# Attention in rounds of four heads: turning half a round ahead, three shared two-bank places, last keys' scores as four 64x64 tiles, segments of one tiling each

## The chip, the cores and the metric

The kernel runs on one core of a Trainium2 chip. The metric is the device time of one execution in microseconds (us), as the median of several runs. A core has five engines that run their own queues of instructions in order: PE (matrix products and transposes, writing PSUM), DVE (vector work), ACT (activations and copies), POOL (vector work that reads and writes SBUF) and SP, which here only issues DMAs. PSUM has eight banks of 512 floats per partition.

## The reference, cut to what matters

The program is an attention layer with a sigmoid in place of a softmax, followed by two dense layers. The change is in the attention alone.

```python
q, k, v: (4 batches, 12 heads, 448 positions, 64)      # float32
scores = scale * np.matmul(q, k.transpose(0, 1, 3, 2)) - np.log(S)
attn = 1.0 / (1.0 + np.exp(-scores))
x = np.matmul(attn, v)          # heads side by side: (1792, 768)
x = square(relu(x @ w_in)) @ w_out                      # 768 -> 2048 -> 768
x = (max(h, 0) + alpha * min(h, 0)) @ w2_out, h = x @ w2_in
```

The weights arrive as 64-bit floats and are turned into 32-bit ones on the chip.

## The kernel before

**Units and rounds.** A unit u is a pair of heads of one batch; there are 24. Two units, u and w = u + 1, make one pass of the attention loop, called a round here, so there are twelve rounds d = 0 to 11. The 448 keys of a head are three blocks of 128 (r or j = 0 to 2) and a rest of 64.

**Steps of a unit.** `fetch(u)` issues eight DMAs on SP: two each of q and k into the tile `nat`, the last 64 positions of q and k into `qk`, and v into `v` and `vrem`. `turn(u)` transposes q and k with seven matmuls against an identity into one two-bank PSUM tile `tp`; DVE then rounds it into `qkh` (L154) and takes the remainder into `qkl` (L155), so that hi and lo parts together carry full precision. `scores(u, j)` (L165) makes the scores of one block of 128 keys: three products (hi by hi, lo by hi, hi by lo), each for both heads, which are two row halves of the array side by side, a pair of matmuls. For the rest of 64 keys (j = 3) the same three pairs run with 128 columns of weights, of which half are of use. ACT applies the sigmoid to each two-bank result (L174), to `a`, or for the rest to `ar`, which two units share. `values(u, j)` (L183) multiplies the float32 sigmoids of a block with v: the two heads are two column halves of the array, and each float32 matmul stands as two records in the trace. `last_values(d)` (L192) does it for the rests of both units, as four 64x64 tiles at once. `finish(u)` copies the result out of PSUM as `xh` (ACT, L204) and `xl` (DVE, L205), in one or two pieces.

**PSUM.** One place of two banks for `tp`, two places of two banks for scores `sc`, two banks for `av`.

**Order.** The program's order is written by hand and each engine keeps it. In a round PE does two blocks of scores, a block or two of values, a turn, and so on, in eleven segments of one kind each. `turn` of a unit stands directly ahead of the previous unit's last two score blocks, and its DVE work is needed one segment pair later. `finish` of both units stands after `last_values`, ahead of the next turn's DVE work on DVE's queue.

**Weights in the attention.** From round 4 on, `assemble(i)` (ACT L82, DVE L83 to L85) and `split(i-1)` (ACT L95, POOL L96) prepare the first six weight tiles at the round's end, and `split` issues the load of a further tile on SP. The dense layers (L256, L289) follow when the attention is done, and PE works through them without a gap.

Of the kernel before, what the change touches and what calls it, by code (L numbers as in the profile page):

```python
# [9 lines left out]
F32 = mybir.dt.float32  # L10
# [9 lines left out]
def fused_kernel(ctx: ExitStack, tc: tile.TileContext, q, k, v, w1i, w1o, w2i, w2o, alpha, out):  # L20
# [53 lines left out]
    def assemble(i):  # L74

        if i >= len(items):
            return  # L80
        low, high = raws[i][:, :, 0], raws[i][:, :, 1]
        nc.scalar.activation(high.bitcast(F32), high.bitcast(F32), AF.Copy, scale=2.0 ** -112)  # L82
# [26 lines left out]
    with tc.manual_schedule():  # L109
# [5 lines left out]

        with tc.tile_pool(name="apool", bufs=1) as apool, tc.tile_pool(name="apsum", bufs=1, space=bass.MemoryType.PSUM) as psum:
            units = [(b, c) for b in range(B) for c in range(H // 2)]
            NAT = 3
            nats, qks, vals, vrems, parts, sig, avs = {}, {}, {}, {}, {}, {}, {}

            def fetch(u):
                if u >= len(units):
                    return
                b, c = units[u]
                hs = slice(2 * c, 2 * c + 2)
                nats[u] = apool.tile([P, 2, R, 2, D], F32, tag="nat", name=f"nat{u}", bufs=NAT)
                vals[u] = apool.tile([P, 2, R, D], F32, tag="v", name=f"v{u}", bufs=NAT + 1)
                qks[u] = apool.tile([P, 2, D], F32, tag="qk", name=f"qk{u}", bufs=NAT)
                if u % 2 == 0:
                    vrems[u // 2] = apool.tile([P, 2, D], F32, tag="vrem", name=f"vrem{u}", bufs=3)  # L130
                for j, src in enumerate((q, k, v)):
                    if j == 2:
                        nc.sync.dma_start(out=vals[u], in_=src[b, hs, :MAIN, :].rearrange("h (p r) d -> p h r d", r=R))
                    else:
                        for h in range(2):
                            nc.sync.dma_start(out=nats[u][:, j, :, h, :], in_=src[b, 2 * c + h, :MAIN, :].rearrange("(p r) d -> p r d", r=R))
                    last = (qks[u][:REM], qks[u][REM:], vrems[u // 2][half(u)])[j]
                    nc.sync.dma_start(out=last, in_=src[b, hs, MAIN:, :].rearrange("h p d -> p h d"))

            def half(u):  # L140
                return slice(u % 2 * REM, (u % 2 + 1) * REM)

            def turn(u):

                if u >= len(units):
                    return
                ps = psum.tile([P, 1024], F32, tag="tp", name=f"tp{u}", bufs=1)
# [5 lines left out]
                parts[u] = [apool.tile([P, 2 * S], F32R, tag=f"qk{part}", name=f"qk{part}{u}", bufs=2) for part in "hl"]  # L153
                nc.vector.tensor_copy(parts[u][0], ps[:, :2 * S])  # L154
                nc.vector.tensor_sub(parts[u][1], ps[:, :2 * S], parts[u][0])  # L155

            def scores(u, j):

                hi, lo = parts[u]
                at = 512 + j * P if j < R else S - u % 2 * REM  # L160
                ps = psum.tile([P, 2, 512], F32, tag="sc", name=f"sc{u}_{j}", bufs=2)
# [4 lines left out]
                if j < R:  # L166
                    a = sig[u, j] = apool.tile([P, 2, S], F32, tag="a", name=f"a{u}_{j}", bufs=6)
                    at = slice(0, P)
                else:
                    if u % 2 == 0:  # L170
                        sig[u // 2] = apool.tile([P, 2, S], F32, tag="ar", name=f"ar{u}", bufs=2)
                    a = sig[u // 2]
                    at = half(u)
                nc.scalar.activation(a[at], ps[at, :, :S], AF.Sigmoid, bias=bias[at], scale=SCALE)  # L174

            def values(u, j):
                if u < 0:
                    return
                if j == 0:
                    avs[u] = psum.tile([P, 512], F32, tag="av", name=f"av{u}", bufs=2)  # L180
                a, w = sig.pop((u, j)), vals[u]
                for h in range(2):
                    nc.tensor.matmul(avs[u][h * D:(h + 1) * D, :S], w[:, h, j, :], a[:, h, :], start=(j == 0), stop=False)  # L183

            def last_values(d):

                if d < 0:
                    return
                a, w = sig.pop(d), vrems.pop(d)
                for h in range(2):  # L190
                    for u in (2 * d, 2 * d + 1):
                        nc.tensor.matmul(avs[u][h * D:(h + 1) * D, :S], w[half(u), h, :], a[half(u), h, :], start=False, stop=True)  # L192
                finish(2 * d)
                finish(2 * d + 1)

            def finish(u):
                b, c = units[u]
                ps = avs.pop(u)
                for t, (first, n) in enumerate(TILES):
                    lo, hi = max(first, b * S), min(first + n, (b + 1) * S)  # L200
                    if lo < hi:
                        xh, xl = (p[:, lo - first:hi - first] for p in x_tiles(0, t, c))
                        part = ps[:, lo - b * S:hi - b * S]
                        nc.scalar.activation(xh, part, AF.Copy)  # L204
                        nc.vector.tensor_sub(xl, part, xh)  # L205

            fetch(0)
            fetch(1)
            nc.sync.dma_start(out=al, in_=alpha.rearrange("(f p) -> p f", p=P))
            turn(0)  # L210
            for u in range(0, len(units), 2):
                w = u + 1
                scores(u, 0)
                scores(u, 1)
                values(u - 1, 2)
                last_values(u // 2 - 1)
                fetch(u + 2)
                turn(w)
                scores(u, 2)
                scores(u, R)  # L220
                values(u, 0)
                values(u, 1)
                scores(w, 0)
                scores(w, 1)
                values(u, 2)
                fetch(u + 3)
                turn(u + 2)
                scores(w, 2)
                scores(w, R)
                values(w, 0)  # L230
                values(w, 1)

                i = u // 2 - 4
                if u in (2, 4, 6):
                    load(u // 2 - 1)
# [4 lines left out]
            values(len(units) - 1, 2)  # L240
            last_values(len(units) // 2 - 1)


        gpool = ctx.enter_context(tc.tile_pool(name="gpool", bufs=1, reuse_waits="tile"))
# [127 lines left out]
```

## Time and profile before

| what | number |
|---|---|
| median of 3 runs | 1127.27 us (1127.04 to 1127.32) |
| the profiled execution, its own time | 1126.52 us |
| its span in the trace | 1124.7 us |
| PE busy | 1098.4 us, 98% of the span |
| DVE, ACT, POOL busy | 676.2, 361.3, 152.6 us |
| start of the dense layers' first matmul on the chain | 184.56 us |
| granted TensorE clock of the core | 1.00 |

The span is what the trace covers; the execution's own time is 1.8 us more. Busy time is summed over stages with different limits, so the attention (0 to 184.56 us) has to be read by itself.

### The profile page before, as it was taken

To read this page: it belongs to the slowest core of one execution; us is meant where nothing else is said; L and a number is where in the kernel's file an instruction comes from. 1 tells how busy PE (TensorE), PEld (TensorE's weight loads), DVE (VectorE), ACT (ScalarE), POOL (GpSimd) and SP (SyncE) were. 2 spreads that over 40 slices of the span, in tenths; PEclk is the share of its full clock that TensorE was granted. 3 is DMA by queue.
4 is the path that set the end of the run, shared out by engine and by line. 5 is a ranking of instruction groups with operands and counts; after the bars stand their busy time and mean duration, and the time that the engine had idled before them with its cause. 6 is when DMAs were issued, how large, how long until landed. Compare 5 with 4: busy or idle time off the path is not lost.

```text
span 1124.7 us, 14542 instructions
## 1 busy us (share of the span) xinstructions
PE 1098.4 (98%) x5928; PEld 948.1 (84%) x5928; DVE 676.2 (60%) x967; ACT 361.3 (32%) x536; POOL 152.6 (14%) x94
## 2 busy tenths in 40 slices
PE   7999999999999999999999999999999999999998
PEld 4554546898989898989898999999989898989998
DVE  2446662246666666666665765567676767677554
ACT  4667665452322222222224443212121202121110
POOL 0001010010111111111114540102020202010000
PEclk9999999999999999999999999999999999999999
DMA  5763661011121112111212020202020201110014
GB/s 111 174 145 78 155 147 37 1 57 57 57 57 57 57 57 57 57 57 48 66 32 82 29 84 29 85 29 84 26 74 14 84 29 62 51 57 29 1 57 140
DMA packets 89267, 73.31 MB, mean 65 GB/s; under 512 B 52592, under 2 KB 83312, under 8 KB 89200
## 3 DMA queue, kind: packets, MB, share of 16 engines
q1 hardware_dynamic: 89200, 72.38, 22.7%
q8 instruction: 47, 0.77, 0.3%
q14 instruction: 20, 0.16, 0.0%
HBM read 66.85 MB, written 5.51 MB: 64 GB/s over the span
## 4 chain that ended last, share of the span: by engine, by line
PE 87%; DVE 8%; ACT 4%; issue 1%; SPq 0%; DMA 0%; ACTq 0%
PE h L256 39%; PE o L289 38%; PE sc L165 4%; PE av L183 3%; DVE raw L85 2%; DVE raw L84 2%; DVE xl L205 1%; ACT raw L82 1%; DVE qkl L155 1%; DVE qkh L154 1%; ACT xh L204 1%; DVE r L266 1%; DVE g L267 1%; PE tp L149 1%; ACT gh L268 1%; PE av L192 1%
## 5 line engine op out<-in xcount | busy, mean ns | idle before, releaser
L256 PE MATMUL h<-xh,wl 128*128 128x512 f32 (+1 forms) x768 | 278.5, 363 | 0.0
L256 PE MATMUL h<-xl,wh 128*128 128x512 f32 (+1 forms) x768 | 278.3, 362 | 0.0
L256 PE MATMUL h<-xh,wh 128*128 128x512 f32 (+1 forms) x768 | 277.9, 362 | 0.0
L294 DVE TENSOR_TENSOR acc<-o,acc 128x384 f32<-128x384 f32 (+1 forms) x364 | 200.0, 583 | 76.9 <-PE o L289 75.4
L96 POOL TENSOR_TENSOR wl<-raw,wh 128x768 fp32r<-128x768 f32 x64 | 122.3, 1911 | 899.6 <-ACT wh L95 828.9
L256 PEld LDWEIGHTS h<-xh,wh 128*128 128x128 f32 x768 | 144.2, 188 | 15.6 <-issue 0.7
L289 PE MATMUL o<-wh,gh 128*128 128x384 f32 x448 | 150.6, 336 | 6.5 <-DVE acc L294 6.2
L256 PEld LDWEIGHTS h<-xh,wl 128*128 128x128 f32 x768 | 144.1, 188 | 15.1
L256 PEld LDWEIGHTS h<-xl,wh 128*128 128x128 f32 x768 | 144.1, 188 | 15.0
L289 PE MATMUL o<-wl,gh 128*128 128x384 f32 x448 | 149.9, 335 | 0.0
L289 PE MATMUL o<-wh,gl 128*128 128x384 f32 x448 | 149.8, 334 | 0.0
L289 PE MATMUL o<-gh,wl 128*128 128x512 f32 (+1 forms) x384 | 139.1, 362 | 0.0
L289 PE MATMUL o<-gl,wh 128*128 128x512 f32 (+1 forms) x384 | 139.0, 362 | 0.0
L289 PE MATMUL o<-gh,wh 128*128 128x512 f32 (+1 forms) x384 | 138.9, 362 | 0.0
L268 ACT ACTIVATE gh<-g 128x512 fp32r<-128x512 f32 (+1 forms) x64 | 37.0, 579 | 284.8 <-DVE g L267 284.8
L269 DVE TENSOR_TENSOR gl<-g,gh 128x512 fp32r<-128x512 f32 (+1 forms) x128 | 93.2, 728 | 52.6 <-ACT gh L268 45.7
L95 ACT ACTIVATE wh<-raw 128x768 fp32r<-128x768 f32 x64 | 57.3, 895 | 174.9 <-DVE raw L85 129.0
L263 DVE SCALAR_TENSOR_TENSOR g<-h,r 128x512 f32<-128x512 f32 (+1 forms) x64 | 39.9, 623 | 112.7 <-ACT r L262 112.7
L84 DVE SCALAR_TENSOR_TENSOR raw<-raw 128x768 int32<-128x768 int32 x64 | 81.0, 1266 | 36.2 <-ACT raw L82 32.3
L262 ACT ACTIVATE r<-h 128x512 f32<-128x512 f32 (+1 forms) x64 | 34.8, 543 | 184.9 <-PE h L256 184.3
L289 PEld LDWEIGHTS o<-wh,gh 128*128 128x128 f32 x448 | 84.1, 188 | 9.3 <-DVE acc L294 8.1
L174 ACT ACTIVATE a<-sc,bias 128x896 f32<-128x896 f32 x72 | 70.0, 1005 | 51.9 <-PE sc L165 51.5
(44 smaller groups left out, 1185.1 us busy)
## 6 DMA issues: line engine op xcount, KB each, us to landing
raw<-in_moe_w_in_dram SPq DMA_DIRECT2D x32, 768.0 KB, 4.8
raw<-in_moe_w_out_dram SPq DMA_DIRECT2D x32, 768.0 KB, 4.4
nat<-in_q_dram SPq DMA_DIRECT2D x48, 96.0 KB, 3.2
nat<-in_k_dram SPq DMA_DIRECT2D x48, 96.0 KB, 2.9
v<-in_v_dram SPq DMA_DIRECT2D x24, 192.0 KB, 2.8
out_dram<-acc SPq DMA_DIRECT2D x16, 192.0 KB, 2.7
out_dram<-acc SPq DMA_DIRECT2D x6, 384.0 KB, 2.3
qk<-in_q_dram SPq DMA_DIRECT2D x24, 32.0 KB, 2.6
```

The costliest lines, as they stand in the source:

```text
L84: nc.vector.scalar_tensor_tensor(out=low, in0=high, scalar=3, in1=low, op0=ALU.logical_shift_left, op1=ALU.bitwise_or)
L95: nc.scalar.activation(hi, w, AF.Copy)
L96: nc.gpsimd.tensor_sub(lo, w, hi)
L165: nc.tensor.matmul(ps[:, h, :S], kt[rows, at:at + P], qt[rows, :S], start=(i == 0), stop=(i == 2))
L174: nc.scalar.activation(a[at], ps[at, :, :S], AF.Sigmoid, bias=bias[at], scale=SCALE)
L256: nc.tensor.matmul(ps[:, :n], wp[:, c * P:(c + 1) * P], xp, start=(c == 0 and i == 0), stop=(c == NC - 1 and i == 2))
L262: nc.scalar.activation(r, ps[:, :n], AF.Relu)
L263: nc.vector.scalar_tensor_tensor(out=gt, in0=ps[:, :n], scalar=0.0, in1=r, op0=ALU.max, op1=ALU.mult)
L268: nc.scalar.activation(gh, gt, AF.Copy)
L269: nc.vector.tensor_sub(gl, gt, gh)
L289: nc.tensor.matmul(ps[:, :size], *ops, start=(i == 0), stop=(i == len(turns) - 1))
L294: nc.vector.tensor_add(part, ps[:, :size], part)
```

## The change

The attention is written anew as rounds of two units. The main points, in the words of the code:

- `fetch(d)` loads both units of a round; it is issued for round d + 2 in the middle of round d, behind both turns. `nat` and `qk` have two places in place of three.
- `turn` of both units of round d + 1 stands in the middle of round d. DVE copies the transposes out of PSUM as float32 (`flat`), and makes the hi part (`part`) and the lo part (`rest`) later from this SBUF copy.
- The scores of the last 64 keys of four heads are one group, `last_scores(d)`: four float32 matmuls straight from `flat`, each in its own 64x64 tile, and one sigmoid of 128x896 in place of two of 64x896.
- One PSUM tag `big` of three two-bank places serves turns and scores alike, nine uses a round.
- `values(u)` does all three blocks at once. A round is last scores and last values, three blocks of scores, three of values, two turns, three of scores, three of values.
- `assemble` is cut in two: its ACT part stands in round i + 4, its DVE part (`step` 1) at the head of the next round.

```diff
-                nc.vector.tensor_copy(parts[u][0], ps[:, :2 * S])
-                nc.vector.tensor_sub(parts[u][1], ps[:, :2 * S], parts[u][0])
+                flats[u] = apool.tile([P, 2 * S], F32, tag="flat", name=f"flat{u}", bufs=2)
+                nc.vector.tensor_copy(flats[u], ps[:, :2 * S])
+            def part(u):
+                parts[u] = [apool.tile([P, 2 * S], F32R, tag=f"qk{p}", name=f"qk{p}{u}", bufs=3) for p in "hl"]
+                nc.vector.tensor_copy(parts[u][0], flats[u])
+            def rest(u):
+                nc.vector.tensor_sub(parts[u][1], flats[u], parts[u][0])
...
+            def last_scores(d):
+                ps = big(f"scr{d}").rearrange("p (h s) -> p h s", h=2)
+                for h in range(2):
+                    rows = slice(h * D, (h + 1) * D)
+                    for u in (2 * d, 2 * d + 1):
+                        nc.tensor.matmul(ps[half(u), h, :S], flats[u][rows, S:S + REM], flats[u][rows, :S], start=True, stop=True)
+                sig[d] = apool.tile([P, 2, S], F32, tag="ar", name=f"ar{d}", bufs=2)
+                nc.scalar.activation(sig[d], ps[:, :, :S], AF.Sigmoid, bias=bias, scale=SCALE)
...
+            for d in range(ND):
+                u, w = 2 * d, 2 * d + 1
+                i = d - 4
+                last_scores(d)
+                if d:
+                    last_values(d - 1)
+                    finish(u - 2)
+                if 0 < i < 7:
+                    assemble(i - 1, 1)
+                for j in range(R):
+                    scores(u, j)
+                if d:
+                    values(w - 2)
+                if d + 1 < ND:
+                    turn(u + 2)
+                    turn(w + 2)
+                    fetch(d + 2)
+                if d:
+                    finish(w - 2)
+                if d + 1 < ND:
+                    part(u + 2)
+                    rest(u + 2)
+                    part(w + 2)
+                    rest(w + 2)
+                if d in (1, 2, 3):
+                    load(d - 1)
                 if 0 <= i < 6:
-                    assemble(i)
+                    assemble(i, 0)
                 if 0 < i < 7:
                     split(i - 1)
+                for j in range(R):
+                    scores(w, j)
+                values(u)
+            last_values(ND - 1)
+            finish(2 * ND - 2)
+            values(2 * ND - 1)
+            finish(2 * ND - 1)
```

On PE, this is the program before, around the last keys' scores of unit 9 (`sc9_3`, three pairs) and the values that follow; a number behind a name is the unit, then the block.

```order
L165 MATMUL sc9_2_811<-qkh9_741 128x448 x2
L165 MATMUL sc9_2_811<-qkl9_742,qkh9_741 128x448 x2
L165 MATMUL sc9_2_811<-qkh9_741,qkl9_742 128x448 x2
L165 MATMUL sc9_3_820<-qkh9_741 128x448 x2
L165 MATMUL sc9_3_820<-qkl9_742,qkh9_741 128x448 x2
L165 MATMUL sc9_3_820<-qkh9_741,qkl9_742 128x448 x2
L183 MATMUL av9_828<-a9_0_775,v9_639 64x448 x2
L183 MATMUL av9_828<-a9_1_784,v9_639 64x448 x2
L165 MATMUL sc10_0_837<-qkh10_807 128x448 x2
```

The same place of PE in the changed program, the head of round 5: `scr5` are the last keys' scores of units 10 and 11, L204 the last values of round 4.

```order
L196 MATMUL av8_831<-a8_2_738,v8_486 64x448 x2
L186 MATMUL scr5_838<-flat10_754 64x448
L186 MATMUL scr5_838<-flat11_764 64x448
L186 MATMUL scr5_838<-flat10_754 64x448
L186 MATMUL scr5_838<-flat11_764 64x448
L204 MATMUL av8_831<-ar4_700,vrem4_484 64x448
L204 MATMUL av9_845<-ar4_700,vrem4_484 64x448
L204 MATMUL av8_831<-ar4_700,vrem4_484 64x448
L204 MATMUL av9_845<-ar4_700,vrem4_484 64x448
L176 MATMUL sc10_0_859<-qkh10_795 128x448 x2
L176 MATMUL sc10_0_859<-qkl10_796,qkh10_795 128x448 x2
```

Twelve matmuls for the last keys of two units (three pairs each) have become four, beside the last values, which use tiles of the same size.

On DVE, this is one weight round before, from the turn of unit 12 to the turn of unit 13 and its parts.

```order
L154 CAST qkh12_959<-tp12_951 128x896
L155 TENSOR_TENSOR qkl12_960<-tp12_951,qkh12_959 128x896
L83 TENSOR_SCALAR raw1_537<-raw1_537 128x768
L84 SCALAR_TENSOR_TENSOR raw1_537<-raw1_537 128x768
L85 SCALAR_TENSOR_TENSOR raw1_537<-raw1_537 128x768
L205 TENSOR_TENSOR xl0_0_4_564<-av10_915,xh0_0_4_563 128x64
L205 TENSOR_TENSOR xl0_1_4_1022<-av10_915,xh0_1_4_1021 128x384
L205 TENSOR_TENSOR xl0_0_5_568<-av11_980,xh0_0_5_567 128x64
L205 TENSOR_TENSOR xl0_1_5_1028<-av11_980,xh0_1_5_1027 128x384
L154 CAST qkh13_1051<-tp13_1043 128x896
L155 TENSOR_TENSOR qkl13_1052<-tp13_1043,qkh13_1051 128x896
```

The same round of DVE in the changed program, from the finish of unit 10 on.

```order
L215 TENSOR_TENSOR xl0_1_4_1005<-av10_983,xh0_1_4_1004 128x384
L86 TENSOR_SCALAR raw1_519<-raw1_519 128x768
L87 SCALAR_TENSOR_TENSOR raw1_519<-raw1_519 128x768
L88 SCALAR_TENSOR_TENSOR raw1_519<-raw1_519 128x768
L159 COPY flat14_1052<-tp14_1044 128x896
L159 COPY flat15_1062<-tp15_1054 128x896
L215 TENSOR_TENSOR xl0_0_5_648<-av11_997,xh0_0_5_647 128x64
L215 TENSOR_TENSOR xl0_1_5_1090<-av11_997,xh0_1_5_1089 128x384
L164 CAST qkh14_1093<-flat14_1052 128x896
L167 TENSOR_TENSOR qkl14_1094<-flat14_1052,qkh14_1093 128x896
L164 CAST qkh15_1097<-flat15_1062 128x896
L167 TENSOR_TENSOR qkl15_1098<-flat15_1062,qkh15_1097 128x896
```

The parts now stand last, read SBUF alone, and are for units of the round after; the finish of the second unit has come to stand behind both copies `flat`.

## Rows read from the trace of the kernel before

**Rows 1.** Page, busy us and share of the span by engine, with instructions

```profile
PE 1098.4 (98%) x5928; PEld 948.1 (84%) x5928; DVE 676.2 (60%) x967; ACT 361.3 (32%) x536; POOL 152.6 (14%) x94
```

**Rows 2.** Chain that ended last, 0 to 330 us: start, us, engine, tile, line

```profile
26.47 0.91 PE av L192 x8
...
28.30 1.42 PE sc L165 x12
29.71 1.65 PE av L183 x8
...
32.78 0.90 PE av L183 x4
...
39.98 0.91 PE av L192 x8
...
67.03 0.98 PE av L192 x8
...
171.66 0.98 PE av L192 x8
...
181.24 2.40 PE av L183 x12
...
184.56 16.54 PE h L256 x72
```

**Rows 3.** The same chain in the round from 67 us on

```profile
68.50 0.50 ACT xh L204
...
73.01 1.29 PE sc L165 x8
```

**Rows 4.** Timeline of PE, 28 to 42 us: start, us, line, operation, tiles

```profile
28.74 0.36 PE L165 MATMUL sc<-qkh,qkl 64*128 64x448 f32 x2
28.94 0.37 PE L165 MATMUL sc<-qkh 64*128 64x448 f32 x2
...
33.61 0.55 PE L149 MATMUL tp<-eye,nat 128*128 128x128 f32 x3
34.00 0.27 PE L150 MATMUL tp<-eye,qk 128*128 128x128 f32 x1
34.10 0.49 PE L152 MATMUL tp<-eye,nat 128*128 128x128 f32 x3
34.53 0.47 PE L165 MATMUL sc<-qkh 64*128 64x448 f32 x2
```

**Rows 5.** Timeline of DVE, 60 to 125 us

```profile
81.01 0.96 DVE L85 SCALAR_TENSOR_TENSOR raw<-raw 128x768 int32<-128x768 int32 x1
...
90.62 1.09 DVE L154 CAST qkh<-tp 128x896 fp32r<-128x896 f32 x1 [3.20 <-PE tp L152]
...
95.48 2.53 DVE L85 SCALAR_TENSOR_TENSOR raw<-raw 128x768 int32<-128x768 int32 x1
```

**Rows 6.** Timeline of POOL, 60 to 195 us

```profile
95.34 1.85 POOL L96 TENSOR_TENSOR wl<-raw,wh 128x768 fp32r<-128x768 f32 x1 [94.04 <-ACT wh L95]
```

**Rows 7.** Timeline of ACT, 80 to 115 us

```profile
88.25 1.91 ACT L174 ACTIVATE a<-sc,bias 128x896 f32<-128x896 f32 x2 [1.77 <-PE sc L165]
...
94.36 0.91 ACT L95 ACTIVATE wh<-raw 128x768 fp32r<-128x768 f32 x1
```

**Rows 8.** Timelines of SP's DMA queue: start, us to issue

```profile
21.33 0.62 SPq L138 DMA_DIRECT2D qk<-in_k_dram  x1
...
102.95 1.23 SPq L136 DMA_DIRECT2D nat<-in_q_dram  x2
...
107.51 0.62 SPq L138 DMA_DIRECT2D vrem<-in_v_dram  x1
```

**Rows 9.** DMA issues, 20 to 180 and 58 to 66 us: KB, median us to landing

```profile
qk<-in_k_dram SPq DMA_DIRECT2D x21, 32.0 KB, 2.9
...
nat<-in_q_dram SPq DMA_DIRECT2D x3, 96.0 KB, 5.0
```

**Rows 10.** Timeline of PE near the start

```profile
13.12 0.84 PE L152 MATMUL tp<-eye,nat 128*128 128x128 f32 x3
```

More of the change, by code (lines that the diff above doesn't have):

```diff
@@ L72, in load, with assemble @@
             nc.sync.dma_start(out=d, in_=w[f * P:(f + 1) * P, :])
-    def assemble(i):
+    def assemble(i, step=None):
         if i >= len(items):
@@ L81, in assemble @@
         low, high = raws[i][:, :, 0], raws[i][:, :, 1]
-        nc.scalar.activation(high.bitcast(F32), high.bitcast(F32), AF.Copy, scale=2.0 ** -112)
+        if step != 1:
+            nc.scalar.activation(high.bitcast(F32), high.bitcast(F32), AF.Copy, scale=2.0 ** -112)
+        if step == 0:
+            return
         nc.vector.tensor_scalar(out=low, in0=low, scalar1=29, scalar2=None, op0=ALU.logical_shift_right)
@@ L117, in fused_kernel @@
             units = [(b, c) for b in range(B) for c in range(H // 2)]
[L118 to L138, printed above, removed]
@@ L140, in half, with fetch @@
+            ND = len(units) // 2
+            nats, qks, vals, vrems, flats, parts, sig, avs = {}, {}, {}, {}, {}, {}, {}, {}
             def half(u):
                 return slice(u % 2 * REM, (u % 2 + 1) * REM)
+            def fetch(d):
+                if d >= ND:
+                    return
+                vrems[d] = apool.tile([P, 2, D], F32, tag="vrem", name=f"vrem{d}", bufs=3)
+                for u in (2 * d, 2 * d + 1):
+                    b, c = units[u]
+                    hs = slice(2 * c, 2 * c + 2)
+                    nats[u] = apool.tile([P, 2, R, 2, D], F32, tag="nat", name=f"nat{u}", bufs=2)
+                    vals[u] = apool.tile([P, 2, R, D], F32, tag="v", name=f"v{u}", bufs=5)
+                    qks[u] = apool.tile([P, 2, D], F32, tag="qk", name=f"qk{u}", bufs=2)
+                    for j, src in enumerate((q, k, v)):
+                        if j == 2:
+                            nc.sync.dma_start(out=vals[u], in_=src[b, hs, :MAIN, :].rearrange("h (p r) d -> p h r d", r=R))
+                        else:
+                            for h in range(2):
+                                nc.sync.dma_start(out=nats[u][:, j, :, h, :], in_=src[b, 2 * c + h, :MAIN, :].rearrange("(p r) d -> p r d", r=R))
+                        last = (qks[u][:REM], qks[u][REM:], vrems[d][half(u)])[j]
+                        nc.sync.dma_start(out=last, in_=src[b, hs, MAIN:, :].rearrange("h p d -> p h d"))
@@ L143, in turn, with big @@
+            def big(name):
+                return psum.tile([P, 1024], F32, tag="big", name=name, bufs=3)
             def turn(u):
-                if u >= len(units):
-                    return
-                ps = psum.tile([P, 1024], F32, tag="tp", name=f"tp{u}", bufs=1)
+                ps = big(f"tp{u}")
                 for r in range(R):
@@ L165, in scores @@
                         nc.tensor.matmul(ps[:, h, :S], kt[rows, at:at + P], qt[rows, :S], start=(i == 0), stop=(i == 2))
[L166 to L181, printed above, removed]
-                for h in range(2):
-                    nc.tensor.matmul(avs[u][h * D:(h + 1) * D, :S], w[:, h, j, :], a[:, h, :], start=(j == 0), stop=False)
+                sig[u, j] = apool.tile([P, 2, S], F32, tag="a", name=f"a{u}_{j}", bufs=5)
@@ L185, in last_values, with values @@
+            def values(u):
+                for j in range(R):
+                    a = sig.pop((u, j))
+                    if u % 2 == 0 and j == 0:
+                        avs[u] = psum.tile([P, 512], F32, tag="av", name=f"av{u}", bufs=2)
+                    for h in range(2):
+                        nc.tensor.matmul(avs[u][h * D:(h + 1) * D, :S], vals[u][:, h, j, :], a[:, h, :], start=(u % 2 == 0 and j == 0), stop=(u % 2 == 1 and j == R - 1))
             def last_values(d):
-                if d < 0:
-                    return
@@ L189, in last_values @@
-                a, w = sig.pop(d), vrems.pop(d)
+                a, w, u = sig.pop(d), vrems.pop(d), 2 * d
+                avs[u + 1] = psum.tile([P, 512], F32, tag="av", name=f"av{u + 1}", bufs=2)
                 for h in range(2):
[L191 to L194, printed above, removed]
+                    for i in (u, u + 1):
+                        nc.tensor.matmul(avs[i][h * D:(h + 1) * D, :S], w[half(i), h, :], a[half(i), h, :], start=(i > u), stop=(i == u))
@@ L209, in fused_kernel @@
[L209 to L235, printed above, removed]
+            nc.sync.dma_start(out=al, in_=alpha.rearrange("(f p) -> p f", p=P))
@@ new lines, in fused_kernel @@
+            for u in (0, 1):
+                turn(u)
+                part(u)
+                rest(u)
+            fetch(1)
+            for d in range(ND):
[24 more added lines that the diff above has]
+                    load(d - 1)
@@ L236, in fused_kernel @@
                 if 0 <= i < 6:
-                    assemble(i)
+                    assemble(i, 0)
                 if 0 < i < 7:
                     split(i - 1)
-            values(len(units) - 1, 2)
-            last_values(len(units) // 2 - 1)
+                for j in range(R):
+                    scores(w, j)
[4 more added lines that the diff above has]
+            finish(2 * ND - 1)
         gpool = ctx.enter_context(tc.tile_pool(name="gpool", bufs=1, reuse_waits="tile"))
```

13 lines of the change are left out of this document (7 added, 6 removed).

## The prediction

> **What bounds the kernel now.** I read the page first, then the chain that ended last, then the engines' timelines in the attention. PE is busy for 98% of the span [rows 1], so time is won only where PE gets less to do or waits less. The chain shows both kinds of loss in the attention. From 26.47 to 39.98 us it runs on PE alone: a whole round between two blocks of last values, 13.51 us without a wait [rows 2]. From 67.03 to 171.66 us there are seven rounds, 104.63 us, where seven of 13.51 would be 94.6; so about 10.1 us there are waits. Their pattern is seen after 68 us: PE has finished the last values, the chain leaves PE for the copies out of `av` on ACT and DVE and the parts of the next turn, and PE's scores return to it at 73.01 [rows 3]. The dense layers start at 184.56 [rows 2]; nothing behind that is edited, and I take it as unchanged. The question is when they start.
>
> **PE's work in a round.** All on PE, so all of it on the path. Before, a segment of two score blocks (six pairs) is 1.41 us from its start to the next segment, two blocks of values are 1.66, one is 0.90, the last values are 0.91 [rows 2], a turn is 0.92, from 33.61 to 34.53 [rows 4]. A round has four, two, two, one and two of these: 5.64 + 3.32 + 1.80 + 0.91 + 1.84 = 13.51, which is the round that the chain shows.
>
> Inside a segment a pair of score matmuls comes 0.20 us after the one before, and a transpose 0.10 to 0.11 after the one before [rows 4]. So 6 pairs are 1.2 us, and 0.2 is the change from one tiling to the next. After, a block of scores adds three pairs to a segment: 1.41 + 0.61 = 2.02. Three blocks of values are 2.40 us as the chain has them at 181.24 [rows 2]. Two turns in one segment are 0.92 + 7 x 0.107 = 1.67. The last values stay 0.91.
>
> The four float32 matmuls of the last keys' scores are not in the trace of before. The nearest row is that of the last values: four float32 matmuls of 64x64 tiles on 448 columns, eight records, 0.91 us with the change of tiling [rows 2]. The upper bound is that they run one after another. A block of values, two matmuls side by side, adds 1.65 - 0.90 = 0.75 us, so four in a row would be 3.0. Shape and type are those of the last values, and I take 0.76, behind which the last values follow in the same tiling: 0.91 + 0.76 = 1.67 for both. The round is then 1.67 + 2 x 2.02 + 2 x 2.40 + 1.67 = 12.18 us, or 1.33 less. About 0.46 of this is the last keys' scores (six pairs, 1.22 us, become 0.76), and the rest is five fewer changes of segment.
>
> **Waits that the new order makes.** Let t be the end of the first turn of a round. DVE copies it until t + 1.1 (a copy of 128x896 out of PSUM is 1.09 us [rows 5]) and the second until t + 2.2. PE needs 0.75 for the second turn and 1.3 for the next two blocks of scores (six pairs and the change of tiling), and the third block wants the PSUM place of the second turn: PE is there at t + 2.05, and waits about 0.2. I charge this in the ten rounds 1 to 10.
>
> In the weight rounds 5 to 9, ACT has a longer queue. The finish of the second unit goes copy, remainder, copy; its first remainder stands on DVE behind both `flat` copies, at t + 2.2. A whole finish takes 1.4 us (two of them and two passes of 1.09 fill the time from 68.01, the end of the last values, to 73.01 [rows 2, 3, 5]); of this ACT still needs some 0.75, with a copy of 0.50 in it [rows 3], and is through at t + 2.95. Then come two weight passes of 0.9 [rows 7] and the first sigmoid of the second unit, about 1.0 (two are 1.91 [rows 7]). That ends at t + 5.8. The next round's last scores take the PSUM place of this sigmoid; PE comes to it at t + 0.75 + 2.02 + 0.2 + 2.40 = t + 5.4. So another 0.4 or so of wait in five rounds; I take 0.45. In rounds 1 to 4 and 10 one or both weight passes are missing and it is hidden. Behind a waiting PE nothing is lost on other engines but their own idle time.
>
> **What lies beside PE.** Two sigmoids of 64x896 become one of 128x896, a sigmoid's time less on ACT each round, hidden anyway. DVE had four passes of 1.09 a round for two turns and now has six, two `flat` copies out of PSUM and four parts out of SBUF: 2.2 us a round more at most. In the light rounds DVE's slack covers it: the parts are wanted by the next round's scores, at about t + 7, and DVE is done with those of the first unit at t + 2.2 + 0.7 + 2.2 = t + 5.1.
>
> In weight rounds POOL's pass comes beside them. At 95.48 a DVE pass of two SBUF inputs took 2.53 us while POOL ran its 1.85 us pass from 95.34 on, against 0.96 us without POOL [rows 5, 6]. So the parts can be held up to about 1.6 us a round. The Trainium skill says of this (SBUF — State Buffer, section "Who interferes with whom") that a DVE instruction with two SBUF inputs contends with a GpSimd instruction that reads SBUF, the later one blocking until the first is done. The trace agrees with it, 2.53 us against 0.96, and by it the parts, which now read SBUF only, are exposed where the passes of before, which read PSUM, were not.
>
> Without that hold DVE's round is at most 2.8 (two finishes, with the hops to ACT) + 2.2 (`flat`) + 4.4 (parts, each bounded above by the PSUM pass of 1.09) + 2.9 (weights, three passes of at most 0.96 [rows 5]) = 12.3 us, under a round of 12.83. With the hold it is 13.9, over it. The lower end is 0: finishes wait for ACT with DVE idle, so a part of the 2.8 can slide under the rest, and each pass is at its bound in this sum. I charge nothing, since parts are due half a round after they are made, and keep the upper end for a rival.
>
> **DMAs.** A unit's eight issues take 5.2 us on SP, from 102.95 to 108.1 [rows 8]. `nat` has two places now, so the loop is: turn done, first unit's issues 5.2, the second's up to its last part of k 3.25, landing 2.9 [rows 8, 9], in all 11.4 us, and PE comes to it a round and 0.4 us later. That is 12.8 against 11.4: hidden with about 1.4 to spare.
>
> **The start.** SP's order at the start is as before. The last part of k of unit 3 is issued at 21.33 and lands 2.9 us later, at 24.2 [rows 8, 9]. PE now needs it in round 0, since the turns stand ahead of the second unit's scores. Three more transposes, 2.02 of scores and 2.40 of values bring round 1 to 29.2 us. PE stands idle ahead of 24.2, and before 15 us the three transposes took 0.84 against 0.49 later [rows 4, 10]. If all of this runs at that pace it is 3.4 more; if none, 0. Some idle time is sure, its effect is not, and I take 1.0: 30.2 us.
>
> **Sum.** Rounds 1 to 4 and 10 at 12.18 + 0.2 = 12.38: 61.9. Rounds 5 to 9 at 12.83: 64.2. Round 11 has no turn: 10.5. The tail of last values and values is 0.91 + 2.40 = 3.3. The dense layers then start at 30.2 + 61.9 + 64.2 + 10.5 + 3.3 = 170.1 us, 14.5 earlier than 184.56. The profiled execution took 1126.52 us, so 1112.0; its time lies 0.75 under the median of the runs, and I say 1112.5.
>
> **Rivals.**
> 1. DVE becomes the bound of the weight rounds, by the hold of POOL: for it speaks the 2.53 us row, against it the slack between parts and scores. Rounds 5 to 9 become 13.4 to 13.9 and PE waits for `flat` or the parts: 3 to 5 us more, about 1117. Chance 0.2. The rule of the Trainium skill named above (SBUF — State Buffer, "Who interferes with whom") would make it this.
> 2. The fetch loop becomes the bound: transfers land later beside a weight load, 5.0 us at 58 to 66 us [rows 9]. With 5.0 the loop is 13.5, a round of 13.1, which is 0.3 to 0.7 more in up to nine rounds with a weight load: 3 to 6 us, about 1117. Against it: the load is issued behind both units' transfers, so it delays the first ones of the next round, which have time. Chance 0.13.
> 3. Slower: the four score tiles do not run side by side. At 3.0 in place of 0.76 it is 2.24 in each of twelve rounds, 27 us, about 1139. It decides from 0.76 + 14.5/12 = 1.97 us a group on. Against it is the row of the last values, the same shape in 0.91. Chance 0.04.
> 4. None of the waits that I charge appear, and PE runs at full pace from the start: 10 x 0.2 + 5 x 0.45 + 1.0 = 5 less, about 1107. It lies inside the range.
>
> **How the numbers follow.** My forecast has 0.6, with its own range of 1107 to 1116; rivals 1 and 2 reach to 1119 or so. The range is 1106 to 1119, which leaves out rival 3 and the ends of 2. A measurement of this kernel tells about 0.2%, 2.3 us, from no change. Rivals 1 and 2 and the forecast are all faster by more than that; same and slower are left to rival 3, to rivals 1 and 2 together at more than their prices, and to what I have not seen: 0.93, 0.02, 0.05.
>
> **What would show it.** Last scores and last values as one stretch of about 1.67 us, at a distance of 12.2 to 12.4 us between rounds up to about 80 us; first round at 29 to 31 us; rounds of some 12.8 between 80 and 145 us, with PE waiting for ACT's sigmoid at the last scores and for `flat` at the third block; the dense layers' first matmul at about 170 us and as long from there to the end as before. It is wrong if PE waits for `nat` at the turns in the middle of the run, if the parts are waited for, or if a group of last scores takes over 1.9 us.

## The result and the profile after

The changed kernel takes **1112.39 us** (median of 4 runs, 1111.45 to 1112.73) against 1127.15 us (4 runs, 1126.53 to 1127.32) in the same comparison. The ratio is 0.9869, 95% interval 0.9852 to 0.9886. The forecast was 1112.5 us. The profiled execution took 1112.57 us, its span is 1110.8 us.

The page, busy time and share of the span, beside [rows 1]:

```profile
PE 1087.2 (98%) x5880; PEld 942.4 (85%) x5880; DVE 691.8 (62%) x991; ACT 347.7 (31%) x524; POOL 154.5 (14%) x94
```

PE has 48 matmuls and 11.2 us of busy time less, and still 98%. The chain that ended last, 0 to 320 us, answers to [rows 2]: start, us, engine, tile, line.

```profile
25.52 3.66 PE sc L176 x18
29.17 2.81 PE av L196 x12
31.98 0.91 PE scr L186 x8
32.90 0.75 PE av L204 x8
33.65 2.02 PE sc L176 x18
35.67 2.41 PE av L196 x12
...
106.84 0.91 PE scr L186 x8
...
112.93 0.48 PE tp L154 x3
...
114.61 1.41 PE sc L176 x12
...
116.02 0.88 PE sc L176 x6
116.90 2.41 PE av L196 x12
119.31 0.91 PE scr L186 x8
...
156.71 0.91 PE scr L186 x8
...
170.54 16.55 PE h L276 x72
```

A round now begins at `scr`, the last keys' scores. The one from 106.84 to 119.31, a round with weights, is 12.47 us: 0.91 last scores, 0.75 last values, 2.02 scores, 2.41 values, 1.68 for the two turns (112.93 to 114.61), 2.29 for the second unit's scores (1.41 + 0.88), 2.41 values. All of it is PE; only the 2.29 has a wait in it, 0.27 over the 2.02 of the other segment. Rounds 1 to 10 together go from 31.98 to 156.71, 124.73 us or 12.47 each: the rounds with weights are no longer than the light ones. The dense layers begin at 170.54 instead of 184.56 [rows 2], 14.02 us earlier, and last as long as before: 940.26 us to the end of the span, 940.14 before.

The first two rows are the surprise: round 0's second scores and values took 3.66 and 2.81 us where later ones take 2.02 and 2.41. The stretches there show why; columns are the stretch, its length, busy time of PE, PEld, DVE, ACT and POOL (instructions), granted clock, DMA share, GB/s.

```profile
22.00:24.00 2.00, 0.52 (x3) 0.31 (x3) 0.00 (x0) 0.00 (x0) 0.00 (x0) 0.78 0.56 122
24.00:26.00 2.00, 1.57 (x8) 1.23 (x10) 0.45 (x1) 0.00 (x0) 0.00 (x0) 0.50 0.58 149
26.00:28.00 2.00, 2.00 (x14) 1.80 (x12) 1.97 (x3) 1.01 (x1) 0.00 (x0) 0.50 0.54 122
...
30.00:32.00 2.00, 2.00 (x16) 0.59 (x16) 0.00 (x0) 1.01 (x1) 0.00 (x0) 1.00 0.46 109
```

PE stood nearly still before, waiting for the loads of unit 3, as its timeline shows (in brackets the idle time just before, and its releaser):

```profile
22.09 0.52 PE L154 MATMUL tp<-eye,nat 128*128 128x128 f32 x3 [1.59 <-DMA nat<-in_q_dram]
24.43 0.45 PE L155 MATMUL tp<-eye,qk 128*128 128x128 f32 x1 [1.82 <-DMA qk<-in_k_dram]
```

The granted clock is 0.50 (1.2 of 2.4 GHz) from 24 to 30 us and 1.00 after.

This start is that of one execution. Experiments 5, 6 and 7 below leave everything ahead of round 1 as it is, and round 1 begins at 30.47, 30.19 and 30.55 us in them, where it is 31.98 here: the load that PE waits for came 0.5 to 0.9 us earlier, and the clock was low for some 3 to 4 us, not 6. The chain of experiment 6:

```profile
24.21 3.24 PE sc L176 x18
...
30.19 0.91 PE scr L186 x8
```

DVE in a round with weights, beside [rows 5], and POOL's pass in it, beside [rows 6]:

```profile
113.88 2.09 DVE L159 COPY flat<-tp 128x896 f32<-128x896 f32 x2 [0.43 <-PE tp L157]
...
117.08 0.62 DVE L164 CAST qkh<-flat 128x896 fp32r<-128x896 f32 x1
117.73 1.09 DVE L167 TENSOR_TENSOR qkl<-flat,qkh 128x896 fp32r<-128x896 f32 x1
118.74 2.28 DVE L164 CAST qkh<-flat 128x896 fp32r<-128x896 f32 x1
```

```profile
118.36 2.18 POOL L99 TENSOR_TENSOR wl<-raw,wh 128x768 fp32r<-128x768 f32 x1 [10.23 <-ACT wh L98]
```

Two things are to be seen. A cast from SBUF is 0.62 us alone and 2.28 us beside POOL: the one at 118.74 ends at 121.02, half a microsecond behind POOL's pass (120.54). The Trainium skill (SBUF — State Buffer, "Who interferes with whom") says that a cast that uses both of DVE's port pairs and a GpSimd instruction shut each other out for the whole instruction; the trace agrees, 2.28 us against 0.62. That this cast uses both pairs is not shown by a run, only that it is held. And ahead of the `flat` copies DVE waited 0.43 us for PE's turns: the only time in this round when it waited for PE, and so the slack that is to be seen there.

### The profile page after: what moved, and what is told of

Same layout as the page of the kernel before. It is cut to its first block, busy times and chain, and to the rows that moved or that the text cites. A ratio compares the mean times of both kernels' runs of the same rounds, so it can differ in the third digit from the quotient of the medians.

```text
span 1110.8 us, 14450 instructions
## 1 busy us (share of the span) xinstructions
PE 1087.2 (98%) x5880; PEld 942.4 (85%) x5880; DVE 691.8 (62%) x991; ACT 347.7 (31%) x524; POOL 154.5 (14%) x94
## 4 chain that ended last, share of the span: by engine, by line
PE 92%; DVE 4%; ACT 2%; SPq 1%; DMA 0%; issue 0%; ACTq 0%
PE h L276 40%; PE o L309 39%; PE av L196 5%; PE sc L176 5%; DVE raw L87 1%; SPq L142 1%; PE scr L186 1%; PE av L204 1%; DVE r L286 1%; PE tp L154 1%; DVE g L287 1%; PE tp L157 1%; ACT gh L288 1%; DVE raw L88 1%; ACT raw L83 1%; ACT wh L98 1%
## 5 line engine op out<-in xcount | busy, mean ns | idle before, releaser
L87 DVE SCALAR_TENSOR_TENSOR raw<-raw 128x768 int32<-128x768 int32 x64 | 81.1, 1267 | 30.1 <-ACT raw L83 25.7
L286 DVE TENSOR_SCALAR r<-h,al 128x512 f32<-128x512 f32 (+1 forms) x64 | 43.6, 681 | 71.4 <-PE h L276 71.3
```

Of the source, the lines that this page charges most:

```text
L286: nc.vector.tensor_scalar(out=r, in0=ps[:, :n], scalar1=0.0, scalar2=al[:, f:f + 1], op0=ALU.min, op1=ALU.mult)
```

## The experiments

The question was which parts of the forecast were right for the right reason: four score tiles side by side, parts made from SBUF, turns together, and slack left on DVE and in the loads. Each edit below is against the changed kernel, and none leaves out a part of the reference. "Rounds" are distances from one `scr` to the next. An edit that adds lines shifts the line numbers, so go by the tiles' names.

Each run was compared with the kernel before in its own session, where that took 1126.1 to 1126.4 us and not 1127.15, so a difference to 1112.39 us is good to about 1 us. The start, as shown above, differs by 1.4 to 1.8 us between traces that share it. For small differences the stretch from round 1's `scr` to the dense layers is the better measure: 138.56 us in the changed kernel (31.98 to 170.54).

**1. Parts made from PSUM.** Both parts and the copy are made behind the turn, all three out of its PSUM place.

```diff
 (in turn)
+                parts[u] = [...]
+                nc.vector.tensor_copy(parts[u][0], ps[:, :2 * S])
+                nc.vector.tensor_sub(parts[u][1], ps[:, :2 * S], parts[u][0])
                 nc.vector.tensor_copy(flats[u], ps[:, :2 * S])
 (part, rest)
+                pass
```

> The changed kernel with one part undone: DVE makes both parts and the copy straight from the transposes in PSUM, three passes of about 1.09 us a unit one after another, so a turn's place is held three times as long. Theory (the early copy to SBUF is what keeps DVE's work on the turns off PE's path): PE's second block of scores of the second unit wants the first turn's place, free at t + 3.3 where PE is there at t + 1.4, and the third block the second turn's place, free at t + 6.6 where PE is there at t + 2.1; about 4.4 us more wait in each of eleven rounds, 45 to 50 us in all, about 1160 us, slower than the kernel before. Rival (the gain is only PE's smaller work, and DVE has slack enough in any order): within 5 us of the changed kernel's 1112.4.

Measured: 1160.07 us, ratio 1.0303 (1.0286 to 1.0320). The total is as expected, its distribution not. Its chain in one light round and the one after:

```profile
57.88 0.91 PE scr L187 x8
...
66.55 1.02 ACT a L179
...
71.49 0.91 PE scr L187 x8
...
78.53 1.10 DVE qkh L159
...
85.02 1.49 PE sc L177 x6
...
90.33 0.91 PE scr L187 x8
```

From 71.49 on PE waits for six DVE passes (three for each turn, the first of the six shown; 78.53 to 84.87) and a round is 18.2 to 19.7 us, 6 to 7 more; the round before is 13.61, only 1.14 more. In the round from 71.49 the two waits are 4.0 us (1.84 and 2.14 on PE's timeline), near the 4.4 expected; most of the rest is PE's slower pace behind them, at a granted clock of 0.50 from 84 to 88 us. That the total fits is luck: three light rounds grew by 1.14 each, and the later ones by more than 4.4. The built program tells why the light rounds are short (the words in brackets name the engine whose progress a matmul waits for). Of the second unit's blocks of scores in that light round, the second waits for ACT (it was given the place of the block just ahead of it, so it waits for that sigmoid) and only the third for DVE; in the next round both wait for DVE, having been given the two places of the turns:

```
L177 MATMUL sc7_1_670<-qkh7_486 128x448 [waits Activation_49]
L177 MATMUL sc7_2_679<-qkh7_486 128x448 [waits DVE_49]
...
L177 MATMUL sc9_1_813<-qkh9_626 128x448 [waits DVE_49,PE_49]
L177 MATMUL sc9_2_822<-qkh9_626 128x448 [waits DVE_49,PE_49]
```

So which of the three shared places a block gets is not a fixed rotation. In the changed kernel's program both blocks wait for DVE in every round that has turns, as the prediction had it. What follows: with turns in the same places as scores, what DVE does between a turn and giving its place free is on the path, and one copy instead of three passes is worth nearly all of these 48 us.

**2. The last scores as before.** Three pairs for each unit in a PSUM place of its own, and two sigmoids.

```diff
 (in last_scores)
+                    hi, lo = parts[u]
+                    at = S - u % 2 * REM
+                    for i, (kt, qt) in enumerate(((hi, hi), (hi, lo), (lo, hi))):
+                        for h in range(2):
+                            nc.tensor.matmul(ps[:, h, :S], kt[rows, at:at + P], qt[rows, :S], ...)
```

> The changed kernel with the last keys' scores undone: three pairs with 128 columns of weights for each unit, and two sigmoids of 64x896, at the head of the round. Theory (the four tiles save 0.46 us of PE and one change of tiling a round, and reading the float32 copy lets them start before the parts are ready): 0.6 us more in twelve rounds, 7 us, and in the six weight rounds, where the second unit's low part is done 2.9 us into the round, another 1 to 2 us each, so 1125 to 1132 us in all. Rival (four tiles run no faster than the pairs): 1112 to 1114.

Measured: 1138.79 us, 1.0113 (1.0098 to 1.0128). Light rounds are 13.13 us, 0.66 more, as expected. Rounds with weights grew by 2.9 to 4.4, where at most 2.6 was expected. Its chain there:

```profile
113.71 1.10 DVE qkl L167
...
114.86 0.68 PE scr L190 x3
```

In the last three of them about 1.5 us is PE's slower pace behind the wait (granted clock 0.50 from 116 to 118 us). A round now opens with the parts of its second unit, which DVE makes last, so PE waits for DVE and DVE then for PE's turns: a closed loop. In the changed kernel the last scores read `flat` alone, which is ready half a round earlier. That is a gain of the four-tile form that the prediction did not name, larger in these rounds than the 0.66 us on PE. The edit also makes ten uses of the three shared places a round in place of nine; what that alone costs was not tested.

**3. q's and k's last rows loaded twice.**

```diff
 (in fetch)
+for _ in range(1 if j == 2 else 2):
     nc.sync.dma_start(out=last, ...)
```

> The changed kernel with the two small loads of q and k of each unit issued twice, 1.3 us more of SP's queue a unit, 2.6 us a round. Theory (the loop of a turn, the next round's loads and the next turn has only about 1 us to spare): PE waits for loads at the turns, 1 to 2 us in each of ten rounds, 10 to 20 us and some at the start, 1122 to 1135. Rival (loads have much to spare): 1113 to 1115, by the start alone.

Measured: 1228.66 us, 1.0909 (1.0889 to 1.0929), far outside. SP's queue shows that this was another experiment than meant (start, us to issue):

```profile
68.68 3.05 SPq L145 DMA_DIRECT2D qk<-in_k_dram  x2
```

Two issues side by side took 1.23 us in [rows 8]. The second load of the same tile waited until the first had landed, four times a round: the built program makes SP wait for the first load's semaphore. It tells nothing of spare time in the queue.

**4. Two idle loads a unit.** The same count of issues, of 16 KB each, into a tile that nobody reads.

```diff
 (in fetch)
+if j < 2:
+    pad = apool.tile([REM, D], F32, tag="pad", ..., bufs=2)
+    nc.sync.dma_start(out=pad, in_=src[b, 2 * c, MAIN:, :])
```

> The changed kernel with two more loads of 16 KB a unit into a place that nothing reads, so that they cost issue time on SP and nothing waits for them; before, doubled loads of one tile waited for each other, and so measured another thing. They add 2.6 us of issue a round. Theory (the loop of turn, loads and next turn has about 1 us to spare, and SP's issues of a round, 10.5 us, about 2): SP's round becomes 13.1 to 13.9 us, PE waits for loads at the turns 0.6 to 1.4 us in each of ten rounds, 6 to 14 us, 1119 to 1127. Rival (loads have room for more): 1112 to 1114, by the start alone.

Measured: 1132.05 us, 1.0055 (1.0042 to 1.0069): 20 us more than the changed kernel, where 6 to 14 were expected. Rounds 1 to 10 take 14.27 us on average (35.76 to 178.42), 1.8 more each; round 1 begins 3.8 later. PE waits for k at the turns, and behind such a stretch the granted clock falls as it does at the start (0.89 in the mean from 92 to 107 us):

```profile
86.73 0.30 PE L158 MATMUL tp<-eye,qk 128*128 128x128 f32 x1 [2.75 <-DMA qk<-in_k_dram]
```

So four more issues a round are enough to put the loads on the path. Without them, k's last piece for unit 9 is issued at 60.42 and, if it lands 2.9 us later [rows 9], is there at 63.3, some 0.9 us ahead of the transpose that reads it (an estimate).

**5. POOL's pass twice** in the six rounds with splits.

```diff
-nc.gpsimd.tensor_sub(lo, w, hi)
+for _ in range(2 if i < 6 else 1):
+    nc.gpsimd.tensor_sub(lo, w, hi)
```

> The changed kernel with POOL's pass issued twice for each of the six weight tiles of the attention, which holds up DVE's SBUF passes about 2 us longer in rounds 5 to 10. Theory (in these rounds DVE has no more than about 1 us of slack left, the parts of the second unit ending 2.9 us into the next round, just when the next finish wants DVE): PE comes to wait for the copies at the third block or for the parts, 1 to 1.5 us in each of six rounds, 6 to 9 us, about 1120. Rival (parts are due half a round later, so that POOL's hold costs nothing even when doubled): 1112 to 1113.

Measured: 1116.86 us, 0.9919 (0.9904 to 0.9934), 4.5 more; 6 to 9 were expected. From round 1 to the dense layers it is 144.02 us, 5.5 more. Five of its rounds with weights average 13.24 us (80.35 to 146.57), 0.78 more, and the chain there runs from DVE to DVE with no PE in it:

```profile
104.80 1.09 DVE qkl L168
105.89 2.21 DVE qkh L165
...
108.12 2.65 DVE qkl L168
```

The second POOL pass holds a second part, 2.65 in place of 1.09 us. That is 1.56 us more in a round, and the round grew by only 0.78; the rest went into idle time that DVE had.

**6. The weights' step left whole**, in place of a part of it moved to the next round.

```diff
-if 0 < i < 7:
-    assemble(i - 1, 1)
 ...
 if 0 <= i < 6:
-    assemble(i, 0)
+    assemble(i)
```

> The changed kernel with the weight step not cut in two: its three DVE passes stand behind the parts at the end of the round, and no longer ahead of the two copies in the middle of the next. Theory (DVE's work of a weight round is the same, but it is now 2.5 us longer after the turns, so the next finish on DVE is late and holds up ACT's sigmoids, which wait behind its second copy): 1 to 1.5 us more of PE wait in five or six weight rounds, 5 to 9 us, 1117 to 1121. Rival (DVE's order inside the round does not matter, its total does): 1112 to 1113.

Measured: 1115.75 us, 0.9905 (0.9890 to 0.9920), a little under the range: six rounds of 13.29 us, 0.8 more each, which is 4.9 from round 1 to the dense layers (143.46); the start of this trace is 1.8 earlier. In its chain the weights' passes stand between the parts and the next finish, and the sigmoid that the turns' place waits for comes behind both:

```profile
107.82 1.09 DVE qkl L167
...
109.49 0.97 DVE raw L87
...
111.44 0.21 DVE xl L215
...
112.01 1.01 ACT a L178
...
113.07 0.55 PE tp L154 x3
```

The cut costs no engine anything and is worth about 5 us in the rounds: it only moves DVE work to where it holds up nobody.

**7. The last values apart from the last scores**, behind the first unit's scores.

```diff
                 last_scores(d)
-                if d:
-                    last_values(d - 1)
-                    finish(u - 2)
 ...
                 if d:
+                    last_values(d - 1)
+                    finish(u - 2)
                     values(w - 2)
```

> The changed kernel with the last values moved behind the first three blocks of scores, so that the round has one more segment of another tiling and the same work. Theory (each change of tiling costs 0.15 to 0.2 us on PE, which is where 0.86 us a round of the gain comes from): 0.15 to 0.2 us more in eleven rounds, about 2 us, 1114.3. Rival (the gain of merged segments is something else, and the order of segments is free): 1112.4.

Measured: 1116.38 us, 0.9912 (0.9898 to 0.9925), 4 us more than the changed kernel, and 143.82 from round 1 to the dense layers, 5.3 more. Its chain:

```profile
55.81 0.91 PE scr L186 x8
...
58.76 0.91 PE av L204 x8
...
68.45 0.91 PE scr L186 x8
...
74.76 0.23 DVE xl L215
...
76.02 2.09 DVE flat L159 x2
...
81.43 0.91 PE scr L186 x8
```

The light round from 55.81 is 12.64 us, 0.17 more than 12.47: the last values cost 0.91 with a change of tiling ahead of them and 0.75 without. The Trainium skill (TensorEngine Tiling (Array Packing), "Key Properties") says that changing the tiling drains TensorE; here that is worth 0.16 us a change. The changed kernel has five fewer changes in a round than the kernel before, some 0.8 us by this price (an estimate); the prediction counted 0.87 for them. The other part was not expected: from 68.45 on rounds are 12.7 to 13.2, since the first unit's finish, which ended well ahead of the `flat` copies on DVE, now ends where they begin: its first piece comes at 74.76, behind a sigmoid on ACT, and the copies at 76.02.

**8. The second `flat` copy on ACT**, half idle in these rounds.

```diff
+                if u % 2:
+                    nc.scalar.activation(flats[u], ps[:, :2 * S], AF.Copy)
+                else:
+                    nc.vector.tensor_copy(flats[u], ps[:, :2 * S])
```

> The changed kernel with the second turn's copy out of PSUM on ACT, which is idle there, in place of DVE. Theory (the third block of scores waits 0.27 us a round for DVE's second copy, nothing else): 0.25 us less in ten or eleven rounds, 2.5 to 3 us, 1109.5 us. Rival (the 0.27 us is a cost of PE's own at this place): no change, 1112.4; or ACT gets late and a sigmoid is waited for: 1113 or more.

Measured: 1108.81 us, 0.9843 (0.9829 to 0.9856), near the 1109.5 expected, though only in part for its reason. Light rounds are 12.19 us, the sum of PE's parts, so the 0.27 us of wait in each of them is the second copy standing behind the first on DVE. From round 1 to the dense layers it is 136.48 us, 2.1 less; round 1 begins at 30.13, and experiments 5 to 7 begin it at 30.2 to 30.6 without this edit.

**9. The first values loaded after q and k of the first four units.**

```diff
 (in words)
-fetch(0); al; turns; fetch(1)
+fetch(0, q and k); turns; fetch(1, q and k); fetch(0, v); al; fetch(1, v)
```

> The changed kernel with another order of the first loads: q and k of the first four units ahead of v and of alpha. Theory (round 1 begins late because the fourth unit's k lands at 24.3 us behind loads that are not needed yet, and PE, idle for it, comes back at a granted clock of 0.50 until about 30 us): k lands some 3 to 4 us earlier, PE is hardly idle, and round 1 begins at 26 us and not at 32; 4 to 6 us less, about 1107. Rival (the start is set by PE's own slow pace, whatever lands when): 1112 to 1113.

Measured: 1109.98 us, 0.9855 (0.9841 to 0.9868), where 4 to 6 less was expected. This interval overlaps the changed kernel's, so a gain is not shown. Round 1 began at 24.10 us, 7.9 earlier, but the wait moved one round on:

```profile
32.15 0.52 PE L159 MATMUL tp<-eye,nat 128*128 128x128 f32 x3 [1.04 <-DMA nat<-in_q_dram]
34.64 0.45 PE L160 MATMUL tp<-eye,qk 128*128 128x128 f32 x1 [1.98 <-DMA qk<-in_k_dram]
```

Units 4 and 5 were now behind four more issues on SP; PE idled, its next scores took 3.66 us again, and round 2 began at 42.49 instead of 44.45. Experiments 5 and 6, with the loads in the old order, reach round 2 at 42.95 and 42.65, so hardly anything of the 7.9 us is left.

**10. Both of the last two.**

> The second copy on ACT and the loads of v behind those of q and k at the start, both as they ran alone. Theory (one is a wait in each round, the other the start, so they add): 1.9 and 3.5 us less than the changed kernel, 1106 to 1107.5 us. Rival (with shorter rounds PE runs into the loads): 1108.8, no better than the copy on ACT alone.

Measured: 1109.0 us, 0.9846 (0.9832 to 0.9859). They do not add. Round 1 begins at 23.64, but round 2 only at 43.29, later than in experiment 9 (42.49) and than in experiment 8 (42.33): what the early start gave is lost again in the same wait for loads. The rounds behind it are 12.2 us.

**11. The first values issued on ACT's queue**, q and k ahead of v throughout, and the copy on ACT.

```diff
 (in words; the copy on ACT is as in 8)
-fetch(0); al; turns; fetch(1)
+fetch(0, q and k); fetch(0, v, on ACT's queue); turns
+fetch(1, q and k); fetch(1, v); al
 (in the loop)
-fetch(d + 2)
+fetch(d + 2, q and k); fetch(d + 2, v)
```

> The changed kernel with the second copy on ACT, and with SP's queue relieved at the start: v of the first round is issued on ACT's queue, and q and k of both units of a round are issued ahead of their v throughout. Theory (in the run with v of two rounds moved back, round 1 began 7.9 us earlier, but the loads for the turns in it were still in SP's queue and gave back 5.9 of it; the queue, not the transfers, sets the start): with 5 us less in that queue ahead of the sixth unit's k, round 1 begins at about 24 us and round 2 about 12.3 us later; about 7 us less from the start and 3.5 from the copy, 1101 to 1103 us. Rival (the transfers themselves are the limit, and v on another queue only delays q and k): 1107 to 1109.

Measured: **1103.28 us** (1103.02 to 1104.08, 5 runs), 0.9795 (0.9782 to 0.9808). This is the best version, and its interval lies clear of the changed kernel's. The first rounds of its chain:

```profile
25.30 0.91 PE scr L194 x8
...
30.14 2.50 DMA qk<-in_k_dram
...
37.85 0.91 PE scr L194 x8
```

Round 2 begins at 37.85, 6.6 us earlier than in the changed kernel and 4.5 earlier than in experiment 8 (42.33), and the granted clock is 1.00 throughout from 14 to 32 us. The chain still goes over SP's queue (27.0 to 30.1) and a load of k there, so issues still bound this round, now by some 0.4 us (12.55 against 12.19). Three edits of the loads act together here (v on ACT's queue at the start, q and k ahead of v in every round, `al` last); which of them gives how much was not tested.

## Why the prediction was right, step by step

The total came out within 0.1 us, and that closeness is luck: in the profiled execution the start was 1.8 us later than forecast and the ten rounds behind it 1.4 us shorter, and the half microsecond added for the median over the profiled execution (1112.0 to 1112.5) was not there (1112.57 profiled, 1112.39 median). What held is the main term, PE's work in a round.

- **PE's work in a round, forecast 12.18.** Right. The pieces measure 1.66, twice 2.02, twice 2.41 and 1.68, together 12.20, and experiment 8 runs light rounds at 12.19 once the wait is gone. The group of four tiles took 0.91 with its change of tiling and the last values behind it 0.75: 1.66 together, forecast 1.67. That the tiles run side by side was the step without a row of its own; rival 3 (3.0 for a group, 1139 us) is out. The two turns in one segment take 1.68, forecast 1.67; no run puts them apart again.
- **The wait of 0.2 for `flat` at the third block.** Right in place, 0.27 in size, shown by experiment 8.
- **The wait of 0.45 for ACT's sigmoid in rounds 5 to 9.** Wrong: it was not there. PE comes to the last scores at 119.31, and the sigmoid whose place they take was over at about 119.2. ACT's timeline (start, us, line, operation):

```profile
116.54 0.93 ACT L83 ACTIVATE raw<-raw 128x768 f32<-128x768 f32 x1
117.36 0.92 ACT L98 ACTIVATE wh<-raw 128x768 fp32r<-128x768 f32 x1
118.19 2.78 ACT L178 ACTIVATE a<-sc,bias 128x896 f32<-128x896 f32 x3
```

  The prediction came to t + 5.8, with t, the end of the first turn, at 113.84 here; measured it is t + 5.3, a tenth ahead of PE. Half of the difference is the finish: the first weight pass starts at t + 2.7 and not t + 2.95. A third is the two weight passes, which start 0.82 us apart though each is listed with 0.92, since neighbours overlap: 1.65 us from the first to the sigmoid, where listed durations gave 1.8. Five rounds of 0.45, 2.25 us, were charged for nothing. Rounds 1 to 10 are 12.20 + 0.27 = 12.47 each, 124.73 in all, against 126.1 forecast.
- **The start, charged 1.0 on top of 29.2.** Under-charged for the profiled execution, where round 1 began at 31.98. Of the 2.78 us over 29.2, 0.23 is the load (24.43 instead of 24.2), and 0.51 + 1.64 + 0.41 are transposes (24.43 to 25.52, 0.58 in the forecast), scores and values at the granted clock of 0.50. In experiments 5, 6 and 7, with the same start, it began at 30.47, 30.19 and 30.55, which is the forecast's 30.2 to within 0.4. So the 1.8 us is in the main a spread between executions, for which the sum had no term. The prediction had the bound for it (3.4 if all of it runs at the pace of [rows 10]; 5.0 us at 0.84 against 0.49 is 3.6) and took a value below the middle.
- **DVE as the bound, rival 1.** It did not come, by about half a microsecond. The cast held by POOL is there in the rounds with weights (2.28), and experiments 5 and 6, which add or move less than 3 us of DVE work, both put DVE on the path and cost about 5 us from round 1 to the dense layers. The prediction's chance of 0.2 was for something that lay that close.
- **The loads, rival 2.** They had about 0.9 us to spare by the estimate above, forecast 1.4; they did not bound the rounds here, and experiment 4 shows how little it takes.
- **Round 11 and the tail, forecast 13.8**, measured 13.83; the dense layers, taken as unchanged, are so within 0.2 us.

## What to carry to other kernels

When two things share a PSUM place, the time from an engine's writing it to the last read can come onto the path, as it did here: copy it out in one pass and do the rest from SBUF, and keep what opens a round off what is made last. Add up neighbouring instructions of an engine start to start, since their listed durations overlap. When PE must stand still for loads near the start, price the half round after it at either clock, as a range, and judge a change in the rounds by the rounds and not by the total, since the start can differ by more. Look at the queue that issues the loads too: here moved loads gave 4.5 us in the traces and 5.5 in the medians (1108.81 to 1103.28), about a third of what the whole change did, while the order alone (experiment 9) showed no clear gain.

## What the runs showed of the hardware that was not expected

- After PE had worked little from 20.5 to 24.4 us its granted clock was 0.50 from 24 to 30 us, and this cost 2.04 us in scores and values alone. In experiment 6, with the same program up to there, the clock was low from about 24 to 28 us and the two took 1.5 us more than at full clock (3.24 + 2.73 against 2.02 + 2.41). The same came in experiment 9 (0.50 from 34 to 38 us, behind the two waits shown there), and not in experiment 11, where PE was busy from 14 to 32 us.
- POOL's own pass took 2.18 us beside a DVE cast from SBUF, 1.85 before [rows 6]. It starts 0.46 us before DVE's pass of two SBUF inputs ends (117.73 + 1.09); whether that or the cast holds it was not tested.
- A DVE cast of 128x896 is 0.62 us from SBUF and was 1.09 from PSUM [rows 5], so of the four parts in a round the two casts are cheaper than the bound of the prediction.
